# One kernel of attention and two feed-forward layers, with all its instructions in another program order

## The chip, the cores and the metric

The kernel runs on one core of one Trainium2 chip. The metric is the device time of one execution in microseconds (us). The core has a matrix engine (TensorE, PE in the rows; PEld is its weight load), a vector engine (DVE), a scalar engine (ACT), GpSimd (POOL) and a sync engine (SP), whose queue issues nearly all DMA transfers here (SPq in the rows). Each engine takes its instructions in the order in which the program lists them; an instruction that waits for another engine holds up all that stand behind it on its own.

## The reference

```
attn = window attention: q_l, k_l, v_l (4, 8, 512, 64), 32 global rows q_g, k_g, v_g per head
       (local rows see |i - j| <= 32 and the global rows; global rows see all; softmax with max)
x    = attn as (2176, 512)                                       # 4 * (512 + 32) rows
h    = max(max(x @ w1, x @ w2), x @ w3);  x = h @ w_out          # w1..w3 (512, 768), w_out (768, 512)
out  = (sigmoid(x @ w_gate) * (x @ w_val)) @ w_out2              # (512, 1536), (1536, 512)
```

All is float32. w1 to w_out2 arrive as float64, two 32-bit words for a number.

## The kernel before, in words

**Attention** goes by 32 units `t` of one batch, one half of the sequence and one pair of heads (labels "sc" scores, "sm" softmax, "av" the product with v; "smg", "avg" for the global rows, whose scores are `sgs`, maxima and sums `stg` and exponents `eg`). The first eight units (batch 0) transpose on TensorE.

**The max layer** goes by 8 chunks `c` of 256 or 288 rows. For each of six slabs `f` of 128 hidden columns and each of w1 to w3, `moe1_l1` (L877) makes one product into one of three PSUM banks (L882 for chunk 0, whole float32; L321 to L323, three products of high and low parts, for the others); ACT (L890) or DVE (L893, L896) takes it out into `h32`, of which there are two buffers. `moe1_l2` (L909) multiplies by w_out (L918 for chunk 0): one product goes through slabs 0 to 5 of w_out in that order. In the other chunks ACT rounds the high part (L901) and POOL subtracts for the low one (L271), which is the last reader of an `h32` buffer.

**The weights** of this layer come in 24 pieces, `conv_a(i)` (L297): i from 0 to 17 is w1, w2, w3 of slab i // 3, and 18 to 23 are slabs 0 to 5 of w_out. A piece is one load of 512 KB (L302, L305), then four passes of `to_f32` (L281) that make a float32 of a float64: L285 on ACT (even i) or L287 on DVE (odd i), L289 on ACT, L291 and L294 on DVE. Chunk 0 uses what L294 writes. Then ACT rounds (L312) and POOL subtracts (L271) for the chunks after it.

**The gated layer** (`l3_prod` L1023: seven products for each of 36 units, with `snap` L1044 and `l3_out` L1057 to L1065 taking them out) and **the output layer** (`l4_first` L1202, `l4_prod` L1225) follow. Their weights and inputs are prepared by `w_prep` (L985 on), `wo_pre`, `x_prep` (L949, with DVE and ACT passes at L978 and L976) and `g_prep`.

**What sets the order.** Every step of every part is an event. `put` and `once` collect the events with a nominal time; then a table, `ORDER`, says in which order they are carried out, and this order is the program order of each engine:

```
    order = [e[1] for e in sorted(ev, key=lambda e: e[:2])] if ORDER is None else ORDER
    assert sorted(order) == list(range(len(ev)))
    with tc.manual_schedule():
        for n in order:
            ev[n][2]()
```

Buffers are handed out and waits are set as this order makes them needed. The two steps of `moe1_l2` for one output tile `m` are slabs 0 to 4 and then slab 5:

```
        for f in range(NF1):
            if f == NF1 - 1:
                yield
            h = hold["h", f]
```

Of the kernel before, what the change touches and what calls it, by code (L numbers as in the profile page):

```python
# [22 lines left out]
    0, 57, 56, 62, 58, 63, 64, 65, 66, 5, 6, 59, 67, 68, 69, 70, 71, 7, 161, 162, 74, 8, 75, 76, 77, 95, 96, 1861,  # L23
    1862, 72, 163, 164, 165, 166, 1863, 1826, 1827, 1854, 128, 195, 97, 98, 78, 1855, 79, 167, 80, 81, 9, 168, 10, 194,
    169, 170, 173, 60, 1864, 99, 100, 129, 101, 130, 102, 103, 1828, 87, 82, 171, 131, 1829, 104, 1833, 120, 1856,
    1857, 132, 133, 1847, 1896, 107, 83, 121, 122, 84, 1858, 108, 109, 231, 232, 110, 88, 89, 111, 105, 112, 198, 174,
    73, 175, 113, 176, 106, 199, 177, 11, 12, 1840, 61, 186, 13, 14, 1865, 178, 114, 90, 91, 200, 201, 153, 1903, 154,
    123, 155, 279, 15, 16, 115, 116, 117, 172, 1868, 134, 1889, 135, 136, 118, 119, 202, 187, 156, 137, 179, 124, 125,
    188, 233, 1834, 140, 141, 1830, 1848, 1875, 142, 143, 85, 144, 180, 181, 1910, 203, 208, 1831, 157, 234, 235, 182,
    126, 183, 184, 1832, 209, 196, 223, 86, 145, 280, 204, 205, 206, 1849, 92, 1841, 1842, 93, 146, 147, 256, 207, 148,  # L30
    1843, 236, 185, 127, 149, 210, 1850, 1851, 224, 17, 1904, 150, 1897, 1898, 1899, 241, 151, 152, 225, 1882, 257,
    1852, 1835, 189, 190, 281, 1952, 237, 238, 1853, 258, 191, 192, 239, 240, 1866, 94, 158, 159, 160, 1836, 211, 1917,
    1890, 1900, 212, 1876, 197, 138, 213, 242, 1938, 1837, 214, 215, 282, 283, 337, 284, 1877, 1891, 139, 1869, 193,
    1878, 1326, 1322, 1892, 1323, 1905, 1844, 1879, 1880, 243, 1859, 259, 244, 1893, 1906, 338, 339, 1324, 1325, 1327,
    1328, 1314, 1315, 216, 1881, 226, 1845, 1867, 217, 1860, 312, 285, 313, 218, 219, 286, 264, 314, 315, 1894, 1316,
    289, 1895, 287, 245, 288, 246, 247, 1883, 1838, 1931, 1907, 227, 1839, 1338, 316, 317, 248, 291, 292, 265, 1932,
    1870, 396, 249, 250, 1339, 1901, 1918, 318, 1902, 319, 320, 1911, 251, 252, 1340, 1341, 1912, 220, 221, 1884, 1342,
    266, 222, 1933, 267, 1871, 1872, 1885, 304, 1343, 228, 1939, 229, 321, 293, 290, 1330, 360, 1940, 362, 1846, 305,
    1331, 363, 364, 324, 325, 294, 365, 253, 366, 230, 1924, 1332, 367, 1908, 326, 327, 268, 1, 1925, 254, 1926, 1973,
    340, 1913, 1886, 260, 1887, 255, 261, 1953, 262, 1954, 1914, 1909, 1980, 1333, 398, 399, 295, 1941, 269, 270, 271,  # L40
    296, 341, 1981, 400, 401, 1346, 328, 1959, 1317, 1888, 1334, 1318, 1945, 297, 1335, 1919, 18, 1927, 1942, 298, 299,
    468, 1928, 1934, 1350, 1974, 1935, 1347, 1319, 1320, 368, 306, 1354, 1920, 1960, 322, 1975, 19, 402, 403, 1946,
    1947, 1921, 1348, 1321, 2, 1929, 329, 369, 20, 21, 370, 371, 323, 345, 330, 263, 331, 372, 22, 23, 404, 1355, 300,
    272, 273, 274, 24, 1329, 361, 1948, 1966, 1349, 1961, 1962, 1982, 332, 1983, 1984, 1351, 275, 1987, 1930, 25, 1949,
    1344, 1345, 26, 276, 277, 278, 27, 432, 333, 1356, 307, 334, 335, 308, 1955, 336, 373, 1956, 1957, 1958, 388, 1967,
    375, 376, 405, 470, 471, 1968, 472, 1357, 301, 302, 377, 406, 407, 408, 378, 1358, 1359, 389, 1976, 411, 1988, 412,
    342, 28, 346, 1336, 379, 380, 1352, 1353, 4, 1989, 374, 1990, 1991, 3, 1337, 303, 347, 348, 349, 343, 1963, 413,
    1360, 1361, 309, 1985, 1986, 344, 1969, 1970, 1977, 1374, 1362, 434, 435, 310, 1375, 1376, 1366, 414, 350, 351, 29,
    381, 1370, 1371, 382, 1372, 1873, 1367, 352, 383, 353, 1377, 390, 504, 384, 385, 391, 311, 1874, 354, 409, 355,
    1368, 1363, 356, 1992, 386, 357, 1993, 436, 437, 438, 439, 440, 441, 473, 474, 415, 442, 443, 358, 1369, 1364, 359,  # L50
    445, 416, 444, 1964, 1965, 447, 417, 1978, 1386, 1387, 1378, 1922, 418, 419, 397, 424, 1388, 506, 420, 392, 421,
    1380, 1389, 1979, 448, 449, 450, 507, 475, 387, 476, 425, 422, 426, 427, 481, 477, 478, 1379, 678, 508, 509, 451,
    1923, 1381, 510, 479, 480, 483, 1390, 1391, 1392, 1915, 1393, 452, 1936, 1937, 1382, 1383, 511, 512, 1384, 410,
    591, 593, 453, 454, 1385, 594, 1394, 1395, 433, 484, 595, 1396, 485, 1397, 455, 456, 596, 457, 460, 540, 1971, 597,
    458, 513, 514, 423, 515, 516, 1916, 1398, 1410, 1943, 461, 462, 598, 463, 1399, 1972, 393, 1402, 1403, 459, 486,
    482, 487, 446, 488, 394, 1400, 1401, 1411, 542, 1404, 599, 543, 519, 544, 469, 489, 490, 491, 1414, 1405, 464,
    1944, 492, 493, 517, 496, 494, 465, 395, 1412, 520, 497, 1413, 1415, 498, 1416, 428, 499, 1418, 1406, 1407, 600,
    429, 518, 1950, 1417, 545, 601, 1420, 546, 627, 629, 602, 603, 630, 631, 1951, 521, 632, 522, 1373, 1365, 1422,
    1408, 606, 607, 495, 1419, 1421, 466, 430, 431, 523, 608, 524, 1423, 1409, 1424, 1425, 30, 525, 633, 609, 526, 527,
    505, 634, 532, 528, 547, 548, 680, 500, 553, 529, 714, 533, 554, 1426, 1427, 530, 1428, 549, 550, 551, 552, 555,  # L60
    501, 502, 1438, 556, 531, 534, 576, 1439, 681, 682, 577, 1430, 467, 557, 635, 610, 503, 558, 559, 578, 560, 561,
    562, 1429, 683, 579, 1431, 1432, 563, 1466, 640, 1440, 716, 604, 1467, 717, 1442, 1444, 535, 564, 541, 536, 1443,
    611, 612, 613, 718, 565, 566, 568, 1445, 636, 637, 569, 1446, 1468, 1434, 1469, 1447, 1441, 570, 571, 638, 639,
    684, 537, 538, 539, 719, 720, 614, 1470, 615, 1435, 1450, 605, 1436, 567, 1474, 572, 1471, 1472, 580, 581, 582,
    1433, 642, 685, 616, 592, 583, 584, 686, 1448, 1449, 1451, 786, 619, 1473, 617, 687, 618, 1452, 1453, 688, 689,
    620, 621, 622, 623, 1458, 1459, 641, 573, 1460, 643, 644, 645, 1461, 646, 647, 574, 575, 585, 586, 648, 31, 32, 33,
    690, 1462, 1463, 1454, 649, 1464, 650, 1455, 34, 1476, 35, 1456, 1484, 36, 651, 652, 587, 1465, 1475, 1477, 721,
    722, 663, 727, 37, 38, 653, 39, 588, 693, 40, 41, 589, 723, 724, 590, 628, 691, 655, 656, 664, 665, 1478, 1479,
    1480, 694, 666, 1486, 1457, 657, 658, 667, 695, 1481, 696, 697, 1482, 1483, 728, 624, 1485, 788, 698, 625, 1487,
    1488, 1498, 750, 752, 668, 1494, 1489, 1499, 669, 1490, 1491, 753, 1437, 725, 659, 654, 699, 700, 701, 754, 626,  # L70
    726, 789, 790, 702, 1500, 679, 706, 755, 756, 757, 758, 763, 1492, 707, 708, 660, 661, 729, 670, 671, 764, 730,
    1502, 731, 822, 42, 732, 662, 703, 672, 673, 1503, 674, 1501, 733, 709, 675, 676, 1495, 1496, 677, 704, 759, 760,
    761, 762, 765, 1506, 1507, 766, 767, 768, 1530, 734, 1531, 1508, 1509, 1510, 735, 715, 742, 705, 1511, 743, 736,
    824, 737, 825, 1534, 826, 858, 744, 745, 1532, 1512, 791, 792, 738, 1533, 793, 769, 1535, 827, 770, 1513, 1536,
    771, 828, 794, 860, 772, 1537, 861, 862, 863, 1522, 1493, 710, 739, 909, 711, 712, 713, 773, 774, 775, 1504, 1538,
    1540, 776, 795, 796, 797, 798, 1539, 1541, 801, 829, 746, 751, 1514, 692, 778, 779, 1515, 830, 802, 803, 804, 777,
    945, 740, 831, 780, 832, 833, 805, 1516, 1517, 911, 834, 1518, 1519, 1497, 1542, 781, 787, 806, 864, 865, 866,
    1543, 947, 807, 1520, 741, 1544, 808, 1545, 1521, 809, 810, 871, 912, 913, 837, 838, 839, 840, 914, 782, 783, 784,
    1546, 1523, 43, 1524, 872, 814, 835, 811, 812, 813, 867, 868, 1526, 869, 836, 1525, 870, 841, 815, 894, 873, 874,
# [1397 lines left out]
```

## Time and profile before

| | |
|---|---|
| time, median of 3 runs | 837.06 us (834.76 to 839.17) |
| the profiled execution: its time | 835.94 us |
| its span, from the first instruction to the last | 834.2 us |
| TensorE busy, and its mean granted clock | 803.0 us, 0.986 of full |
| DVE, ACT, POOL busy | 603.9, 470.4, 149.2 us |

The span is 1.74 us shorter than the time of the same execution; what lies around it is not seen in the trace. The profiled execution is 1.12 us below the median.

### The profile page before, as it was taken

To read this page: it belongs to the slowest core of one execution; us is meant where nothing else is said; L and a number is where in the kernel's file an instruction comes from. 1 tells how busy PE (TensorE), PEld (TensorE's weight loads), DVE (VectorE), ACT (ScalarE), POOL (GpSimd) and SP (SyncE) were. 2 spreads that over 40 slices of the span, in tenths; PEclk is the share of its full clock that TensorE was granted. 3 is DMA by queue.
4 is the path that set the end of the run, shared out by engine and by line. 5 is a ranking of instruction groups with operands and counts; after the bars stand their busy time and mean duration, and the time that the engine had idled before them with its cause. 6 is when DMAs were issued, how large, how long until landed. Compare 5 with 4: busy or idle time off the path is not lost.

```text
span 834.2 us, 18134 instructions
## 1 busy us (share of the span) xinstructions
PE 803.0 (96%) x6854; PEld 755.6 (91%) x6854; DVE 603.9 (72%) x1303; ACT 470.4 (56%) x1119; POOL 149.2 (18%) x149
## 2 busy tenths in 40 slices
PE   6989699999999999999999999999999999999998
PEld 4768489998989988899999999999999998999998
DVE  5778957756677666875586978989775669987872
ACT  6786556745555555564546766575645366544441
POOL 3142336433323233423140000000000000000000
PEclk9898799999999999999999999999999999999999
DMA  9976435634544555445344345967342369635311
GB/s 204 268 191 184 102 72 99 107 77 98 102 89 87 95 105 111 95 92 93 141 139 134 124 144 171 306 206 240 121 139 70 127 195 350 200 114 171 121 39 44
DMA packets 217590, 116.07 MB, mean 139 GB/s; under 512 B 161056, under 2 KB 204576, under 8 KB 217504
## 3 DMA queue, kind: packets, MB, share of 16 engines
q1 hardware_dynamic: 216960, 114.80, 50.8%
q8 instruction: 53, 0.87, 0.4%
q14 instruction: 33, 0.27, 0.1%
q10 hardware_dynamic: 544, 0.13, 0.1%
HBM read 74.91 MB, written 28.57 MB: 124 GB/s over the span
## 4 chain that ended last, share of the span: by engine, by line
PE 76%; DVE 7%; SPq 6%; DMA 6%; ACT 2%; issue 2%; POOL 1%; POOLq 0%; DVEq 0%; ACTq 0%
PE pa L1038 16%; PE pa L1225 8%; PE ps L321 8%; PE pe L1038 8%; PE ps L323 7%; PE ps L322 7%; PE pe L1225 4%; PE pb L1038 4%; PE pb L1225 2%; DMA m<-in_moe_w_dram 2%; PE sp L619 2%; PE ps L882 2%; SPq L513 2%; PE ps L918 2%; PE ot L780 1%
## 5 line engine op out<-in xcount | busy, mean ns | idle before, releaser
L1038 PE MATMUL pa<-m,m 128*128 128x384 f32 (+1 forms) x864 | 155.5, 327 | 0.9 <-ACT sn L1044 0.9
L321 PE MATMUL ps<-xt,m 128*128 128x288 f32 (+1 forms) x504 | 149.2, 296 | 5.0 <-DVE h L896 3.8
L323 PE MATMUL ps<-xt,m 128*128 128x288 f32 (+1 forms) x504 | 146.6, 291 | 0.0
L1038 PEld LDWEIGHTS pa<-m,m 128*128 128x128 f32 x864 | 144.4, 188 | 2.1 <-ACT sn L1044 2.0
L322 PE MATMUL ps<-xt,m 128*128 128x288 f32 (+1 forms) x504 | 145.1, 288 | 0.0
L321 PEld LDWEIGHTS ps<-xt,m 128*128 128x128 f32 x504 | 94.7, 188 | 12.7 <-DVE h L896 4.8
L322 PEld LDWEIGHTS ps<-xt,m 128*128 128x128 f32 x504 | 94.8, 188 | 0.0
L323 PEld LDWEIGHTS ps<-xt,m 128*128 128x128 f32 x504 | 94.7, 188 | 0.0
L1044 ACT COPY sn<-pa 128x384 f32<-128x384 f32 (+1 forms) x108 | 49.8, 461 | 61.6 <-PE pa L1038 61.3
L1038 PE MATMUL pe<-m,m 128*128 128x384 f32 (+1 forms) x432 | 83.4, 327 | 0.4 <-ACT m L1207 0.4
L1038 PEld LDWEIGHTS pe<-m,m 128*128 128x128 f32 x432 | 72.8, 188 | 0.9 <-ACT m L1207 0.6
L1225 PE MATMUL pa<-m,m 128*128 128x256 f32 x576 | 72.0, 283 | 0.0
L1225 PEld LDWEIGHTS pa<-m,m 128*128 128x128 f32 x576 | 70.4, 192 | 0.0
L896 DVE TENSOR_TENSOR h<-ps,h 128x288 f32<-128x288 f32 (+1 forms) x90 | 38.9, 437 | 40.5 <-PE ps L323 32.8
L661 ACT ACTIVATE sm<-sm,st 128x224 f32<-128x224 f32 x128 | 60.6, 475 | 9.5 <-DVE st L625 9.4
L1163 ACT CAST m<-m 128x768 fp32r<-128x768 f32 x44 | 36.6, 836 | 44.1 <-PE pa L1225 13.9
L271 POOL TENSOR_TENSOR h<-h,h 128x288 fp32r<-128x288 f32 (+1 forms) x42 | 42.1, 1004 | 92.7 <-ACT h L901 88.7
L707 DVE TENSOR_TENSOR pc<-sm,pc 64x512 f16<-64x512 f32 (+1 forms) x72 | 51.5, 715 | 6.6 <-ACT pc L704 5.7
L1168 DVE TENSOR_TENSOR m<-m,m 128x768 fp32r<-128x768 f32 x44 | 41.5, 956 | 18.2 <-ACT m L1163 17.4
L321 PE MATMUL ps<-h,m 128*128 128x288 f32 (+1 forms) x168 | 50.3, 300 | 0.0
L704 ACT CAST pc<-sm 64x512 f16<-64x512 f32 (+1 forms) x72 | 39.2, 545 | 18.0 <-DVE sm L675 17.2
L322 PE MATMUL ps<-h,m 128*128 128x288 f32 (+1 forms) x168 | 48.5, 289 | 0.6 <-POOL h L271 0.6
(194 smaller groups left out, 1632.4 us busy)
## 6 DMA issues: line engine op xcount, KB each, us to landing
m<-in_moe_w_dram SPq DMA_DIRECT2D x18, 512.0 KB, 5.7
gd<-sgt SPq DMA_DIRECT2D x48, 192.0 KB, 2.6
m<-gd SPq DMA_DIRECT2D x6, 1536.0 KB, 8.2
m<-in_moe_w_val_dram SPq DMA_DIRECT2D x6, 1024.0 KB, 5.2
wr<-in_moe_w_out_dram SPq DMA_DIRECT2D x6, 1024.0 KB, 6.3
m<-in_moe_w_gate_dram SPq DMA_DIRECT2D x5, 1024.0 KB, 5.4
vr<-in_v_l_dram SPq DMA_DIRECT2D x48, 96.0 KB, 2.5
x2d<-x2s SPq DMA_DIRECT2D x32, 128.0 KB, 1.9
```

Source lines behind the costliest of these rows:

```text
L271: nc.gpsimd.tensor_tensor(out=out, in0=a, in1=f32(b), op=ALU.subtract)
L321: nc.tensor.matmul(ps, lhsT=wh, rhs=xh, start=first, stop=False)
L322: nc.tensor.matmul(ps, lhsT=wh, rhs=xl, start=False, stop=False)
L323: nc.tensor.matmul(ps, lhsT=wl, rhs=xh, start=False, stop=last)
L661: nc.scalar.activation(sm4[:, i], sm4[:, i], AF.Exp, bias=st[:, 0, i:i + 1], scale=-1.0, accum_out=st[:, 2, i:i + 1])
L704: nc.scalar.copy(d, s_)
L707: nc.vector.tensor_tensor(out=l_, in0=s_, in1=h_, op=ALU.subtract)
L896: nc.vector.tensor_tensor(out=a, in0=ps[:, 0:n], in1=a, op=ALU.max)
L1038: nc.tensor.matmul(ps, lhsT=w[l][:, a, i], rhs=x[m][:, i], start=(k in (1, 2, 5) and i + l + m == 0), stop=(k in (2, 3, 4) and i == 1 and ...
L1044: nc.scalar.copy(t[:, 0:n], pend[u]["a"][:, 0:n])
L1168: tt(out=lo, in0=src[op], in1=f32(hi), op=ALU.subtract)
L1225: nc.tensor.matmul(ps, lhsT=g[l][:, f], rhs=wo_op(b, f, m), start=(k in (1, 2, 5) and f + l + m == 0), stop=(k in (2, 3, 4) and f == 5 and ...
```

## The change

The 3388 numbers of `ORDER` stand in another order; nothing else is changed. 3291 places of the table hold another event than before, and an event stands 19 places from where it stood, in the mean. Instructions, sizes and loads are the same ones; names of buffers are numbered anew in program order.

```
 ORDER = [
-    0, 57, 56, 62, 58, 63, 64, 65, 66, 5, 6, 59, 67, 68, 69, 70, 71, 7, 161, 162, 74, 8, 75, 76, 77, 95, 96, 1861,
...
+    2380, 2381, 3372, 2387, 2303, 3373, 2388, 2389, 2390, 2304, 2391, 2392,
 ]
```

The first place is DVE where TensorE begins the w_out product of chunk 0. Before: slabs 1, 2, 3 and 5 of w_out are m42_889, m45_1057, m39_839 and m46_1072; stg and eg are global rows 7, sm_991 is the softmax of unit 8, xt_1168 the rounding of unit 7.

```order
L724 TENSOR_SCALAR stg_1001<-stg_1001 128x1
L667 RECIPROCAL st_992<-st_992 128x4
L675 TENSOR_TENSOR sm_991<-sm_991,st_992 128x896
L291 SCALAR_TENSOR_TENSOR m46_1072<-m46_1072 128x512
L294 SCALAR_TENSOR_TENSOR m46_1072<-m46_1072 128x512
L731 RECIPROCAL stg_1001<-stg_1001 128x1
L733 TENSOR_SCALAR eg_1002<-eg_1002,stg_1001 128x640
L294 SCALAR_TENSOR_TENSOR m42_889<-m42_889 128x512
L798 SCALAR_TENSOR_TENSOR xt_1168<-ot_1136,xt_1168 128x256
L291 SCALAR_TENSOR_TENSOR m45_1057<-m45_1057 128x512
L294 SCALAR_TENSOR_TENSOR m45_1057<-m45_1057 128x512
L294 SCALAR_TENSOR_TENSOR m39_839<-m39_839 128x512
```

Now slab 2 is m46_1013, slab 3 is m40_821 and slab 5 is m45_1010 (slab 1 is done 26 rows earlier than slab 2, outside these rows), on DVE at the same place:

```order
L291 SCALAR_TENSOR_TENSOR m40_821<-m40_821 128x512
L291 SCALAR_TENSOR_TENSOR m46_1013<-m46_1013 128x512
L294 SCALAR_TENSOR_TENSOR m46_1013<-m46_1013 128x512
L569 STREAM_TRANSPOSE qt_1110<-qr_1023 128x256
L572 STREAM_TRANSPOSE kt_1112<-kgr_527 128x2x32
L574 STREAM_TRANSPOSE kt_1112<-kr_1024 128x64
L576 STREAM_TRANSPOSE kt_1112<-kr_1024 128x2x128
L294 SCALAR_TENSOR_TENSOR m40_821<-m40_821 128x512
L287 TENSOR_SCALAR m45_1010<-m45_1010 128x512
L896 TENSOR_TENSOR h32_1062<-ps1_1088,h32_1062 128x256
L667 RECIPROCAL st_998<-st_998 128x4
L675 TENSOR_TENSOR sm_997<-sm_997,st_998 128x896
```

Twelve steps that stood ahead of slab 3's L294 now stand behind it: L287, L291 and L294 of slab 5, L667 and L675 of unit 8, L731 and L733 of the global rows, L896 and L893 of the last slab of the first layer, two of the score steps (L625) of unit 9, and L798 of unit 7. None has moved ahead of it.

The second place is DVE some 50 us earlier. Before: m35_695 is piece 15 (w1, slab 5) and m27_560 piece 13, the L625 rows are the scores of unit 7.

```order
L724 TENSOR_SCALAR stg_671<-stg_671 128x1
L287 TENSOR_SCALAR m35_695<-m35_695 128x512
L287 TENSOR_SCALAR m27_560<-m27_560 128x512
L625 ISA sm_741,st_742<-sp_704,mask_79 128x224
L625 ISA st_742 128x1
```

Now piece 15 is m36_741 and piece 13 m27_561; L688 takes out transposed softmax:

```order
L287 TENSOR_SCALAR m27_561<-m27_561 128x512
L688 COPY pw_713<-tp_707 128x512
L625 ISA sm_733,st_734<-sp_726,mask_79 128x224
L625 ISA st_734 128x1
L625 ISA sm_733,st_734<-sp_726,mask_79 128x224
L625 ISA st_734 128x1
L625 ISA sm_733,st_734<-sp_727,mask_79 128x224
L625 ISA st_734 128x1
L625 ISA sm_733,st_734<-sp_727,mask_79 128x224
L625 ISA st_734 128x1
L287 TENSOR_SCALAR m36_741<-m36_741 128x512
```

Piece 13, the copy of unit 5 and the four score steps of unit 7 moved ahead of piece 15's first pass. On SP's queue the load of piece 15 moved one place ahead, past that of piece 16, and the load of piece 10 moved from the third of the group issued at 21.9 us to just behind that of piece 8.

The third place is ACT near the end of the max layer, in its last chunk. Before: h_6615 rounds slab 2 (L901), h32_6679 takes out the first product of slab 0 (L890).

```order
L925 COPY x2s_6613<-ps2_6569 128x256
L901 CAST h_6615<-h32_6478 128x288
L976 CAST m75_6619<-m64_6489 128x768
L976 CAST m77_6627<-m60_6442 128x768
L925 COPY x2s_6643<-ps2_6593 128x256
L890 COPY h32_6679<-ps1_6650 128x288
```

Now, with h_6690 for slab 2 and h32_6693 for slab 0:

```order
L289 ACTIVATE m59_6424<-m59_6424 128x1024
L976 CAST m75_6629<-m64_6550 128x768
L976 CAST m77_6634<-m60_6468 128x768
L901 CAST h_6638<-h32_6545 128x288
L925 COPY x2s_6657<-ps2_6612 128x256
L901 CAST h_6690<-h32_6440 128x288
L890 COPY h32_6693<-ps1_6641 128x288
```

The rounding of slab 2 moved behind the casts of `x_prep` and the rounding of slab 1, and stands right ahead of the copy for slab 0.

## Rows read from the trace of the kernel before

**Rows 1.** Windows: busy us and count of each engine, granted clock, DMA share, GB/s.

```profile
0.00:58.00 58.00, 48.17 (x300) 36.48 (x300) 38.45 (x114) 43.72 (x135) 19.28 (x35) 0.94 0.93 233
58.00:118.00 60.00, 49.10 (x337) 39.53 (x337) 47.35 (x117) 32.58 (x91) 15.12 (x12) 0.86 0.47 117
118.00:450.00 332.00, 326.09 (x3670) 303.43 (x3670) 231.62 (x632) 186.99 (x534) 114.82 (x103) 1.00 0.48 99
450.00:831.00 381.00, 379.59 (x2552) 376.20 (x2550) 286.13 (x443) 207.13 (x361) 0.00 (x0) 1.00 0.50 164
```

**Rows 2.** Timeline of PE, 58 to 118 us: start, duration, instructions, idle before and releaser.

```profile
61.97 6.71 PE L882 MATMUL ps<-xw,m 128*128 128x256 f32 x16 [2.83 <-DVE m L294]
...
70.24 5.35 PE L882 MATMUL ps<-xw,m 128*128 128x256 f32 x24
...
92.79 0.71 PE L918 MATMUL ps<-hw,m 128*128 128x256 f32 x2
100.31 1.22 PE L918 MATMUL ps<-hw,m 128*128 128x256 f32 x2 [6.81 <-DVE m L294]
102.78 7.67 PE L918 MATMUL ps<-hw,m 128*128 128x256 f32 x28 [1.26 <-issue]
...
117.74 0.40 PE L321 MATMUL ps<-xt,m 128*128 128x288 f32 x1
```

**Rows 3.** Windows of PE alone, around the first long wait: busy, clock, DMA.

```profile
60.00:65.00 5.00, 3.03 (x7) 0.62 0.57 125
65.00:70.00 5.00, 5.00 (x29) 0.70 0.86 261
```

**Rows 4.** Timeline of DVE, 92 to 104 us.

```profile
92.37 0.38 DVE L896 TENSOR_TENSOR h<-ps,h 128x256 f32<-128x256 f32 x1
...
94.94 1.37 DVE L287 TENSOR_SCALAR m<-m 128x512 int32<-128x512 uint32 x1
...
96.30 0.16 DVE L667 RECIPROCAL st<-st 128x4 f32<-128x4 f32 x1
...
99.57 0.68 DVE L294 SCALAR_TENSOR_TENSOR m<-m 128x512 int32<-128x512 int32 x1
100.17 0.42 DVE L798 SCALAR_TENSOR_TENSOR xt<-ot,xt 128x256 fp32r<-128x256 f32 x1
...
101.99 1.29 DVE L294 SCALAR_TENSOR_TENSOR m<-m 128x512 int32<-128x512 int32 x2
```

**Rows 5.** Timeline of DVE, 53 to 58 us.

```profile
53.43 0.14 DVE L724 TENSOR_SCALAR stg<-stg 128x1 f32<-128x1 f32 x1
57.91 0.76 DVE L287 TENSOR_SCALAR m<-m 128x512 int32<-128x512 uint32 x2 [4.34 <-DMA m<-in_moe_w_dram]
```

**Rows 6.** Timeline of SP's queue, 40 to 50 us: the load of piece 8.

```profile
45.03 0.43 SPq L302 DMA_DIRECT2D m<-in_moe_w_dram  x1
```

**Rows 7.** The line L302 from 20 to 60 us: time to landing.

```profile
DMA to landing us min/median/max: 3.7/6.1/9.3
```

**Rows 8.** The page's costliest groups: busy, mean ns of one, idle before.

```profile
L704 ACT CAST pc<-sm 64x512 f16<-64x512 f32 (+1 forms) x72 | 39.2, 545 | 18.0 <-DVE sm L675 17.2
```

**Rows 9.** Timeline of DVE, 103 to 118 us.

```profile
111.03 0.29 DVE L744 COPY pwg<-tpg 128x128 f32<-128x128 f32 x1 [6.82 <-PE tpg L738]
```

**Rows 10.** Timeline of POOL, 395 to 450 us.

```profile
404.12 0.74 POOL L271 TENSOR_TENSOR h<-h,h 128x256 fp32r<-128x256 f32 x1 [6.30 <-ACT h L901]
416.68 5.24 POOL L271 TENSOR_TENSOR h<-h,h 128x288 fp32r<-128x288 f32 x1 [11.81 <-ACT h L901]
```

**Rows 11.** Timeline of ACT, 405 to 430 us.

```profile
421.95 0.40 ACT L890 COPY h<-ps 128x288 f32<-128x288 f32 x1 [3.59 <-POOL h L271]
```

**Rows 12.** Waits of PE from 450 us on: us in total, times, longest.

```profile
PE pa L1038 <- ACT sn L1044: 0.9, 3, 0.4
PE pe L1038 <- ACT m L1207: 0.4, 1, 0.4
```

**Rows 13.** Waits of SP's own queue over the span: us in total, times, longest.

```profile
SPq L928 <- ACT x2s L925: 61.5, 15, 14.3
```

338 rows, old and new, of the table ORDER are left out of this document.

## The prediction

> **What bounds the kernel now.** I read the windows by stage first [rows 1]. TensorE is busy 803.0 of 834.2 us, so the reader should look for where it is idle, since a change of order alone can take nothing else away. From 0 to 58 us it idles 9.8 us, from 58 to 118 us 10.9, from 118 to 450 us 5.9, from 450 to 831 us 1.4. The first two stretches are 14% of the span and hold two thirds of the idle time; the second also runs at a mean granted clock of 0.86. The last stretch, the gated and output layers, is TensorE work with hardly a gap. The waits of TensorE there [rows 12] are 0.9 and 0.4 us. Whatever the new order does to ACT and DVE there can win about 1 us.
>
> Then I read the timeline of TensorE from 58 to 118 us [rows 2]. Two places wait. At 59.1 us the third product of slab 0 of chunk 0 waits 2.83 us for a weight that DVE finishes with L294, and the 16 matmuls behind it take 6.71 us. At full clock 24 such matmuls take 5.35, so 16 take 3.57: 3.1 us are lost to the clock, which the windows show at 0.62 and 0.70 after the wait [rows 3], between the levels of 1.2 and 2.4 GHz. At 93.5 us the w_out product of chunk 0 waits 6.81 us, starts one tile, and waits 1.26 more: slabs 1, 2 and 3 of w_out come from DVE's L294 one after another, and the last one starts at 101.99 and ends at 103.28 [rows 4]. The 28 matmuls behind it take 7.67 us, where the full rate gives 28 x 0.223 = 6.24, so another 1.4 us are lost. Chunk 1 (L321) can only start at 117.74.
>
> The timeline of DVE shows why the weights are late. From 92 to 103 us it has no idle time [rows 4]: it works, in program order, through steps that nobody waits for before it comes to slab 3. Behind slab 3, with chunk 0 done, it idles 6.82 us at 111.03 [rows 9], so what is put off there has room. Earlier it stood idle 4.34 us for the load of piece 15, up to 57.91 [rows 5], with piece 13 and four score steps queued behind.
>
> **The change, part by part.** The sum is made against the profiled execution, 835.94 us, which is 1.12 below the median of the runs.
>
> *Twelve DVE steps go behind slab 3's L294.* L287 of slab 5 takes 1.36 from its start to the next (94.94 to 96.30); the six consecutive steps L667, L675, L291, L294, L731 and L733 take 3.27 (96.30 to 99.57) [rows 4]. The other five (L896, two of L625, L893, L798) are short; the first and the last of them last 0.38 and 0.42 and overlap their neighbours, so I take 0.32 each, 1.6 together. The sum is 6.2. DVE is dense there, so slab 3 is done 6.2 us earlier. The wait is 6.81 + 1.26 = 8.07, so 1.9 of it stays and the whole 6.2 counts. The product is started by slab 3 in both orders, since slab 5 is used by a second step. The steps put off cost nothing where DVE's idle 6.82 [rows 9] takes them; L291 and L294 of slab 5 are still due before the end of the product, and run while TensorE works its 7 us on slabs 0 to 4. **-6.2.**
>
> *The clock behind that wait.* A shorter wait may lose less. Nothing here shows a wait of 1.9 us in this stretch, so the bounds are 0 (the loss stays 1.4) and -1.4. I take half, **-0.7**. The row of the 2.83 us wait, after which 3.1 were lost [rows 2, 3], speaks against taking it all. The Trainium skill (TensorE: Matmul & The Clock Gate, Part 1: The HAM clock gate) says that throttled is the default state and that activity releases it; the low clock after both waits agrees (0.62 after the first), and by that rule a remaining gap may still be paid for, which is one of the rivals below.
>
> *The load wait of DVE.* Piece 13's first pass (0.76 [rows 5]), a copy and four score steps now stand ahead of piece 15's first pass, and its load is issued one place earlier. Of the wait of 4.34 [rows 5] that can recover up to all. Against it, piece 10's load now follows piece 8's, which is issued at 45.03 [rows 6]; with the median time to landing of 6.1 [rows 7] it is there at 51.1, and two ACT passes stand between it and DVE. That can make DVE wait 1 to 3.4 us in the same stretch. Net I take **-2.0**, bounds 0 and -4.3. DVE is dense from 74 us on, so this goes through to slab 3.
>
> *A new chain behind slab 5.* The reciprocal of global rows 7 (L731) now stands behind slab 5's L294 and waits for an exponential on ACT, which stands behind the copies of unit 8 (L704, 0.545 each [rows 8]). With two of them that is 1.1 us and more, on the way to the last attention product before chunk 1; DVE also has L291 and L294 of slab 5 and some short steps ahead of that product's last step, of the kinds costed above, which I put at 1.7 together. Against that stands the idle 6.82 of DVE [rows 9]. Bounds 0 and 1.1 + 1.7 = +2.8; I take **+1.0**.
>
> *ACT and POOL in the last chunk.* Of `h32` there are two buffers; the copy L890 of slab 0 waits 3.59 for POOL's L271 of slab 2 [rows 11], which takes 5.24 in place of 0.74 when it lies beside a dense run of DVE [rows 10]. It ends just before TensorE needs the bank, and so costs nothing now. In the new order L901 of slab 2 stands last before that copy, behind casts that nobody waits for. If POOL starts that much later, TensorE waits, from 0 up to about the 3.4 that ACT's wait is today. I take **+0.5**, nearer to nothing.
>
> *The gated layer.* A product of the output layer is put ahead of the one that waits 0.4 for ACT's L1207 [rows 12] and covers it: **-0.4**.
>
> *The middle, 118 to 450 us.* TensorE idles 5.9 in all [rows 1], in a handful of waits of 0.5 to 2 us. Every row has moved, by some 19 places in the mean; for each engine the work ahead of a wait changes by tenths of a us up or down. The bounds are -4 (most of the idle goes) and +6 (it doubles); I take **0**.
>
> The sum is -6.2 - 0.7 - 2.0 + 1.0 + 0.5 - 0.4 = -7.8, so 835.94 - 7.8 = 828.1, and with the 1.12 by which the median lies above the profiled execution, **829.2 us**. What this measurement can tell from no change is about 0.5%, 4.2 us: faster means below 832.9, slower above 841.2. The likeliest case's own range is 825 to 832.9: the load wait between 0 and -4.3 and the middle a us or two either way.
>
> **The rivals.**
>
> *More is won.* The whole 4.34 of the load wait is recovered, the wait of 2.83 at 59.1 shrinks with part of its 3.1 of clock loss [rows 2], and the middle loses two of its waits. That is -2.3, -2 and -1 more, 823 to 824. For it speaks that DVE's work before 60 us is reordered too; against it that the first slabs' pieces still go through the same four passes in much the same order. Chance 0.13.
>
> *Half is given back.* Piece 10's late load makes DVE wait the full 3.4 instead of piece 15's, so nothing is won there (+2.0), the clock loss stays (+0.7), and the last chunk waits its full 3.4 (+2.9). With the first alone the time is 831.2, with all three 829.2 + 5.6 = 834.8; with the chain behind slab 5 at its bound too (+1.8) 836.6. The clock alone, if the remaining 1.9 us cost as much as the 2.83 us did (3.1 instead of 0.7), gives 831.6. Chance of 833 to 841: 0.18.
>
> *Slower: SP's queue.* Loads of the next units stand on SP's queue between stores that wait for ACT; the stores wait 61.5 us in all, 14.3 the longest [rows 13]. Today the loads are issued early enough. If the new order puts loads of several units behind a store that waits longer, TensorE waits for scores between 118 and 400 us. From 8 us in all the gain is gone, and from 12 the kernel is slower: with 24 units from there on, 0.5 us for each makes 829.2 + 12 = 841. The order of SP's queue is nearly the same as before and units are loaded with about the same lead, which speaks against it. Chance 0.10.
>
> *The change doesn't reach slab 3*: another wait, of the first layer's last products, holds slab 3's turn anyway. That gives 834 to 836 and is within the second rival's chance.
>
> **How the numbers follow.** The forecast has 0.59, more won 0.13, half given back 0.18, slower 0.10. Faster by over 0.5% is 0.59 + 0.13 = 0.72, no change 0.18, slower 0.10. The range of 8 in 10 leaves out the slower case and the upper part of the second: 823 to 838.
>
> **What the profile after would show.** Right: the wait ahead of the 28 matmuls of L918 is about 2 us in place of 8; chunk 1's first L321 starts at about 110 (117.74 - 6.2 - 0.7 - 2.0 + 1.0 = 109.8); DVE's idle 4.34 and 6.82 are gone or under 3; TensorE's idle time from there to the gated layer is still about 6, and in the gated and output layers about 1. Wrong: a wait of DVE for piece 10's load at 50 us that is as long as piece 15's was; a wait on L731 or L733 in front of chunk 1; a wait for L890 in the last chunk near its slab 0; TensorE waiting for scores or loads of units in the middle. The prediction fails most easily if the 6 us are won in front and the middle or the last chunk, where every row has moved, returns them in waits of 1 to 2 us that no single row of the trace before announces.

## The result and the profile after

The changed kernel took 826.92 us (median of 4 runs, 826.33 to 829.82) beside 836.05 for the kernel before in the same session: ratio 0.9892, 95% interval 0.9864 to 0.992. A second session gave 0.9856 (0.9832 to 0.9879). 829.2 had been forecast, with a range of 823 to 838. The profiled execution has a span of 825.2 us against 834.2, so 9.0 us less, of which TensorE's busy time gives 5.8 (797.2 against 803.0) and its idle time 3.2.

To see where they come from, the two executions are cut at the same places of the program: the first L918 of chunk 0, the first L321 of chunk 1, the last L321 that reads `h`, and the end. These are windows of TensorE of the kernel before (window, length, busy, granted clock, DMA share, GB/s):

```profile
0.00:92.79 92.79, 80.14 (x525) 0.93 0.83 208
92.79:117.74 24.95, 16.89 (x111) 0.79 0.21 46
117.74:448.60 330.86, 324.95 (x3664) 1.00 0.48 100
448.60:834.20 385.60, 380.99 (x2561) 1.00 0.49 162
```

And of the changed kernel:

```profile
0.00:91.37 91.37, 78.88 (x526) 0.98 0.83 212
91.37:107.66 16.29, 15.20 (x112) 1.00 0.35 74
107.66:442.70 335.04, 324.26 (x3671) 0.99 0.47 98
442.70:825.20 382.50, 378.82 (x2554) 1.00 0.50 164
```

Six L1038 stand in the third window after and in the fourth before; they take 1.0 us. With that set right, the start gives 1.4 us, the w_out product of chunk 0 and what leads to chunk 1 give 8.7, the middle takes 3.2 back, and the gated and output layers give 2.1: 1.4 + 8.7 - 3.2 + 2.1 = 9.0.

The traces of the runs below say how firm these are. The second stage took 24.95 to 26.5 us in four executions with the order of before there (before, e2_rest, e3b_gated, e5_piece15) and 16.2 to 16.5 in six with the new one: this is the gain. The 1.4 of the start is not shown: the first L918 came at 90.1 to 93.0 us in six executions whose order up to there is that of before or moves piece 15 alone, and at 91.1 to 95.2 in five with the new one.

The timeline of TensorE after, at the places of [rows 2]:

```profile
54.34 1.09 PE L683 MATMUL tp<-ident,sm 128*128 128x128 f32 x8 [2.76 <-DVE sm L675]
...
63.20 3.73 PE L882 MATMUL ps<-xw,m 128*128 128x256 f32 x16 [0.28 <-DVE m L294]
...
93.55 3.30 PE L918 MATMUL ps<-hw,m 128*128 128x256 f32 x14 [0.61 <-DVE m L294]
97.14 6.29 PE L918 MATMUL ps<-hw,m 128*128 128x256 f32 x28 [0.29 <-issue]
103.45 0.77 PE L738 MATMUL tpg<-ident,eg 128*128 128x128 f32 x5
...
107.66 0.40 PE L321 MATMUL ps<-xt,m 128*128 128x288 f32 x1
```

The waits of 6.81 and 1.26 are now 0.61 and 0.29, the 28 matmuls run at full rate (6.29 for 6.24), and chunk 1 starts at 107.66 where 109.8 was forecast. The wait of 2.83 ahead of piece 6 is 0.28, but one of 2.76 for a softmax (L675) stands at 54 us. In DVE's timeline that L675 takes 2.17 us, where before it took 1.08; POOL works on its L271 beside it, up to 53.3 us:

```profile
52.11 2.17 DVE L675 TENSOR_TENSOR sm<-sm,st 128x896 f32<-128x896 f32 x1
```

The timeline of DVE after, at the places of [rows 4]: slab 3's L294 is done at 93.50 in place of 103.28.

```profile
92.85 0.65 DVE L294 SCALAR_TENSOR_TENSOR m<-m 128x512 int32<-128x512 int32 x1
93.42 0.42 DVE L287 TENSOR_SCALAR m<-m 128x512 int32<-128x512 uint32 x1
...
98.39 0.17 DVE L731 RECIPROCAL stg<-stg 128x1 f32<-128x1 f32 x1 [1.35 <-ACT stg L729]
...
102.85 0.55 DVE L733 TENSOR_SCALAR eg<-eg,stg 128x640 f32<-128x640 f32 x1
```

Windows of DVE up to the end of slab 3, and from 50 to 74 us, first of the kernel before, then of the changed one:

```profile
0.00:103.28 103.28, 79.98 (x218) 0.90 0.76 192
50.00:74.00 24.00, 15.24 (x47) 0.86 0.85 227
```

```profile
0.00:93.50 93.50, 78.37 (x204) 0.98 0.82 208
50.00:74.00 24.00, 21.75 (x53) 0.93 0.69 190
```

Slab 3 comes 9.8 us earlier; only 1.6 of it is busy time, and 8.2 is idle time that DVE no longer has ahead of this place (23.3 before, 15.1 after), 6.5 of it between 50 and 74 us. (That window is one of fixed microseconds. In e2_rest, e4_slabs and e9_both, whose order there is that of before or nearly so, DVE works 18.0 to 18.4 us in it, so some 3 of the 6.5 lie between executions.) The busy time fell by less than the steps that moved behind, since some others took longer beside POOL, among them this L675 and a copy (L410, 1.97 for 0.27); the last experiment comes to that.

The middle after, where TensorE waits (timeline):

```profile
150.63 0.82 PE L780 MATMUL ot<-pt,vb 128*64 128x64 f16 x40 [1.66 <-DVE st L625]
158.79 0.39 PE L321 MATMUL ps<-xt,m 128*128 128x256 f32 x1 [1.38 <-ACT xt L796]
160.61 0.39 PE L322 MATMUL ps<-xt,m 128*128 128x256 f32 x1 [1.43 <-DVE xt L798]
...
223.12 0.61 PE L321 MATMUL ps<-xt,m 128*128 128x288 f32 x1 [2.79 <-ACT h L890]
```

Its idle time is 10.8 us (335.04 - 324.26) where it was 5.9.

### The profile page after: what moved, and what is told of

Read it like the earlier page. It is cut to its first block, busy times and chain, and to the rows that moved or that the text cites. A ratio compares the mean times of both kernels' runs of the same rounds, so it can differ in the third digit from the quotient of the medians.

```text
span 825.2 us, 18078 instructions
## 1 busy us (share of the span) xinstructions
PE 797.2 (97%) x6854; PEld 757.4 (92%) x6854; DVE 610.4 (74%) x1303; ACT 467.0 (57%) x1119; POOL 150.0 (18%) x149
## 4 chain that ended last, share of the span: by engine, by line
PE 71%; DVE 10%; SPq 5%; ACT 5%; DMA 4%; issue 3%; POOL 1%; DVEq 0%; ACTq 0%; POOLq 0%
PE pa L1038 17%; PE pe L1038 8%; PE pa L1225 8%; PE ps L321 6%; PE ps L322 5%; PE ps L323 5%; PE pe L1225 4%; PE pb L1038 4%; PE sp L619 3%; DMA vr<-in_v_g_dram 2%; PE pb L1225 2%; PE ps L882 2%; ACT sm L661 2%; DVE m L978 2%; PE ot L780 1%
## 5 line engine op out<-in xcount | busy, mean ns | idle before, releaser
L321 PE MATMUL ps<-xt,m 128*128 128x288 f32 (+1 forms) x504 | 149.4, 296 | 6.9 <-ACT h L890 4.0
L1038 PE MATMUL pa<-m,m 128*128 128x384 f32 (+1 forms) x864 | 155.7, 327 | 0.3 <-ACT sn L1044 0.3
L1038 PEld LDWEIGHTS pa<-m,m 128*128 128x128 f32 x864 | 144.5, 188 | 0.8 <-ACT sn L1044 0.6
L321 PEld LDWEIGHTS ps<-xt,m 128*128 128x128 f32 x504 | 96.0, 191 | 11.8 <-ACT h L890 5.2
L322 PEld LDWEIGHTS ps<-xt,m 128*128 128x128 f32 x504 | 96.1, 191 | 2.4 <-DVE xt L798 2.0
L323 PEld LDWEIGHTS ps<-xt,m 128*128 128x128 f32 x504 | 96.0, 190 | 0.0
L1038 PE MATMUL pe<-m,m 128*128 128x384 f32 (+1 forms) x432 | 82.0, 327 | 0.0
L1038 PEld LDWEIGHTS pe<-m,m 128*128 128x128 f32 x432 | 72.6, 188 | 0.0
L896 DVE TENSOR_TENSOR h<-ps,h 128x288 f32<-128x288 f32 (+1 forms) x90 | 39.0, 435 | 40.2 <-PE ps L323 28.9
L707 DVE TENSOR_TENSOR pc<-sm,pc 64x512 f16<-64x512 f32 (+1 forms) x72 | 54.2, 752 | 8.0 <-ACT pc L704 6.7
L271 POOL TENSOR_TENSOR h<-h,h 128x288 fp32r<-128x288 f32 (+1 forms) x42 | 41.4, 990 | 90.1 <-ACT h L901 86.1
L625 DVE CUSTOM_DVE_ANT_0 sm<-sp,mask 128x224 f32<-128x224 f32 x128 | 44.7, 383 | 11.1 <-PE sp L619 10.3
L704 ACT CAST pc<-sm 64x512 f16<-64x512 f32 (+1 forms) x72 | 39.2, 546 | 18.4 <-DVE sm L675 16.7
L321 PE MATMUL ps<-h,m 128*128 128x288 f32 (+1 forms) x168 | 49.5, 295 | 0.0
```

The lines of the kernel that those rows point to most:

```text
L271: nc.gpsimd.tensor_tensor(out=out, in0=a, in1=f32(b), op=ALU.subtract)
L321: nc.tensor.matmul(ps, lhsT=wh, rhs=xh, start=first, stop=False)
L322: nc.tensor.matmul(ps, lhsT=wh, rhs=xl, start=False, stop=False)
L323: nc.tensor.matmul(ps, lhsT=wl, rhs=xh, start=False, stop=last)
L625: nc.vector.tensor_tensor_reduce(out=sm[:, hh, j], in0=sp[hh][:, j, 0:224], in1=mask[:, half + j, :], scale=-SC, scalar=3.0e38, op0=ALU.ad ...
L704: nc.scalar.copy(d, s_)
```

## The experiments

All are orders of the same events; none leaves out or changes a part of the computation. Ratios are to the kernel before, run beside each. The numbers in the diffs are those of `ORDER`.

**e1_front and e2_rest: each half of the new order alone.** The first takes the new order up to the first event of chunk 1 and then what is left in the order of before; the second is the reverse.

```diff
 e1_front: the new order up to
     1979, 357,
+    119, 336, 301, 302, 374,      (what is left, as before)
 e2_rest: the order of before up to
     417, 1978,
+    640, 475, 387, 397,           (what is left, in the new order)
```

> The new order up to the first matmul of chunk 1, and behind it what is left in the order of before. Theory (the gain is made in front, and the middle gives 3 us of it back in waits of its own): chunk 1 starts at about 107.7 us as in the changed kernel, and with the old middle its waits of 5.9 us in all come back in place of 10.8, so the time is 10 us below that of before, ratio 0.988, or 1 us below the changed kernel. Rival (the middle's waits follow from what the front leaves behind, whatever the order there): TensorE idles 10 us in the middle here too, and the time is 5 to 7 us below before, ratio 0.992 to 0.994.

> The old order up to the first matmul of chunk 1, and behind it what is left in the new one. Theory: nothing is won in front, the middle costs 3 us and the gated part gives 2 back: 1 us above before, ratio 1.001 (0.998 to 1.005). Rival (the new middle is as good as the old, and its waits come from starting 10 us earlier): 2 us below before, ratio 0.998 and the idle time of TensorE from chunk 1 to the gated part is about 6 us.

e1_front: ratio 0.9897 (0.9876 to 0.9918). e2_rest: 0.9971 (0.9952 to 0.9991). The windows of the middle and of the layers behind it, of e1_front and of e2_rest:

```profile
107.30:440.00 332.70, 325.88 (x3667) 1.00 0.48 99
440.00:825.60 385.60, 380.97 (x2561) 1.00 0.49 162
```

```profile
117.60:447.90 330.30, 322.32 (x3669) 0.99 0.49 100
447.90:830.30 382.40, 378.91 (x2555) 1.00 0.49 164
```

The front holds nearly the whole gain, as expected, and TensorE idles 6.8 us in the middle of e1_front, nearer to the theory's 5.9 than to the rival's 10. But in e2_rest the rival comes nearer: the new middle behind the old front takes 330.3 us, or 329.3 without the six L1038, less than the old one (330.86), while behind the new front it takes 335.0 (334.0). So its extra waits are not in its order alone. Nor do they go by the time at which it starts: in e6_undo12, below, it starts 5.7 us later than in the changed kernel and takes the same 334.9. That the old middle behind the new front takes 332.7 says little, since that order took 330.4 to 333.9 behind the old front (before, e5_piece15, e3b_gated, e12_pool). e2_rest is 2 us faster than before in the time as well, and most of that lies in the gated part (383.4 with the six L1038, against 385.6).

**e3_front_gated and e3b_gated: the three stages recombined.** The first is e1_front with the new order again from the first event of the gated layer; the second changes nothing but that part.

```diff
 e3_front_gated and e3b_gated, behind 2979, 2980:
-    1997, 1824, 2981, 1812,
+    2981, 2982, 2983, 1812, 1813,   (what is left, in the new order)
```

> New order up to the first matmul of chunk 1, the order of before for the middle, and the new one again from the first product of the gated layer on. Theory (three stages whose times nearly add): front as in the changed kernel, middle 2 us shorter than there, as in the run with the new front alone, and the gated part 2 us shorter than before: 11 to 12 us below before, ratio 0.986 to 0.987, the fastest of these orders. Rival (the middle's difference between the two orders is chance of the clock): the same as the changed kernel, ratio 0.989 to 0.990.

> The order of before up to the first product of the gated layer, and behind it what is left in the new order. Theory: the weight loads of TensorE's queue there waited 2.0 us for ACT's L1044 and 0.6 for L1207, of which 1.9 go: the stretch behind the max layer is 2 us shorter and the time 2 us below before, ratio 0.9975, which five rounds may just tell. Rival (only what TensorE itself waited goes, 1 us): ratio 0.999.

e3_front_gated: 0.9883 (0.9862 to 0.9904), e3b_gated: 0.9988 (0.997 to 1.0006). The two theories of each cannot be told apart in the times. The windows can: behind the last L321 of `h`, e3b_gated takes 383.6 us and e3_front_gated 382.9, where six executions with the old order of that part (before, e1_front, e4_slabs, e5_piece15, e9_both, e12_pool) took 384.6 to 386.2. The groups of TensorE's weight loads in this stretch show what went, first before, then in e3b_gated (busy, mean ns, idle time ahead and its releasers):

```profile
L1038 PEld LDWEIGHTS pa<-m,m 128*128 128x128 f32 x864 | 144.4, 188 | 2.1 <-ACT sn L1044 2.0
L1038 PEld LDWEIGHTS pe<-m,m 128*128 128x128 f32 x432 | 72.8, 188 | 0.9 <-ACT m L1207 0.6 <-DVE m L1020 0.3
```

```profile
L1038 PEld LDWEIGHTS pa<-m,m 128*128 128x128 f32 x864 | 144.6, 188 | 0.8 <-ACT sn L1044 0.7
L1038 PEld LDWEIGHTS pe<-m,m 128*128 128x128 f32 x432 | 72.6, 188 | 0.0
```

2.1 + 0.9 - 0.8 = 2.2 us less waiting at the weight loads, and 2.0 less time (385.6 to 383.6). The waits of the matmuls [rows 12] show only 1.3 of it. A wait is longer in the rows of the weight loads than in those of the matmuls: two waits of e4_slabs are 2.42 and 2.00 in the one and 2.02 and 1.63 in the other. In the times themselves e3b_gated is not shown to be faster than before.

**e4_slabs: in the order of before, slabs 1 to 3 ahead of the twelve steps.**

```diff
     1976,                           (slab 3, L291)
+    1963, 1969, 1970, 1977,         (slab 1 L294; slab 2 L291, L294; slab 3 L294)
+    1357, 407, 408, 1359,           (L896, two L625, L893)
```

> The order of before with one edit: the last DVE steps of slabs 1, 2 and 3 of w_out ahead of the twelve steps that the change put behind them. Theory (the 6.2 us of steps were the wait): the waits of 6.81 and 1.26 us ahead of the w_out product fall to 1 to 2 us in all, the 28 matmuls behind them take 6.2 to 7.7, and the time is 6 to 7.5 us below before, ratio 0.991 to 0.993. Rival (the steps put off are waited for at once, as the twelve lie on the way to chunk 1): chunk 1 starts less than 3 us earlier, ratio 0.997 to 1.000.

Ratio 0.9937 (0.9913 to 0.9961). TensorE's timeline:

```profile
92.84 0.71 PE L918 MATMUL ps<-hw,m 128*128 128x256 f32 x2 [2.02 <-DVE m L294]
95.17 7.72 PE L918 MATMUL ps<-hw,m 128*128 128x256 f32 x28 [1.63 <-ACT m L289]
```

The waits fall from 8.07 to 3.65, and the product and what leads to chunk 1 take 20.1 us in place of 24.95. The rival (a start of chunk 1 less than 3 us earlier) falls: 110.2 in place of 117.74. But the theory's 1 to 2 us of waiting were missed, and with them its time. The row names ACT's L289 for the second wait, but no L289 on ACT lies between 94.5 us and TensorE's start at 95.17; that start falls where the first of DVE's two L294 from 94.38 on (slab 2) is done. What made DVE late are POOL's steps beside it (DVE, then POOL):

```profile
91.14 1.64 DVE L294 SCALAR_TENSOR_TENSOR m<-m 128x512 int32<-128x512 int32 x1
92.71 1.64 DVE L291 SCALAR_TENSOR_TENSOR m<-m 128x512 int32<-128x512 int32 x1
94.38 1.29 DVE L294 SCALAR_TENSOR_TENSOR m<-m 128x512 int32<-128x512 int32 x2
```

```profile
90.63 1.61 POOL L593 TENSOR_TENSOR vr<-vr,vb 128x512 f32<-128x512 f32 x1
92.31 1.49 POOL L418 TENSOR_TENSOR vs<-vgr,t 32x512 bf16<-32x512 f32 x1
```

The L294 of slab 1 and the L291 of slab 2 take 1.64 where such steps take 0.69 elsewhere, and slab 3's L291 ahead of them 1.26. An estimate from these rows: the three lose 2.5 us, which leaves 1.2 of the 3.65. The clock gave nothing back either: the 28 matmuls take 7.72, as long as behind the wait of 8.07.

**e6_undo12: the reverse, in the changed kernel.** Slab 3's L294 goes behind the steps again.

```diff
-    1977,                           (slab 3, L294)
...
+    1988, 1357, 1989, 379, 380, 1359, 1990, 1991, 347, 348, 349, 407, 408, 344,
+    1977,
     1374,                           (w_out product)
```

> The changed kernel with one edit: slab 3's L294 on DVE stands again behind the steps that the change put behind it (L287, L291 and L294 of slab 5, L667 and L675 of unit 8, L731 and L733, the takings-out, score steps and L798). Theory: slab 3 is late by these 6.2 us and TensorE waits 6 to 8 us ahead of the w_out product in place of 0.9, with 1.4 of clock behind it: 6 to 8 us above the changed kernel, ratio to before 0.997 to 0.999. Rival (the gain came from DVE no longer standing idle ahead of this place, and not from the steps): at most 3 us above the changed kernel, ratio 0.990 to 0.993.

Ratio 0.9932 (0.9909 to 0.9955), against 0.9892 and 0.9856 for the changed kernel. DVE's row of slab 3 and TensorE's row behind it:

```profile
97.93 0.68 DVE L294 SCALAR_TENSOR_TENSOR m<-m 128x512 int32<-128x512 int32 x1
```

```profile
98.67 10.93 PE L918 MATMUL ps<-hw,m 128*128 128x256 f32 x42 [5.80 <-DVE m L294]
```

Slab 3 is 5.1 us later (97.93 against 92.85), TensorE waits 5.80 in place of 0.90 in all, and the 42 matmuls take 10.93 where the changed kernel needs 3.30 + 6.29 = 9.59 for them: 4.9 + 1.3 = 6.2 us. Chunk 1 starts 5.7 us later (113.35). The wait is just under what was expected (5.80 for 6 to 8) and the clock's share is about as expected (1.3 for 1.4); the ratio lies between the two theories, 3 to 6 us above the changed kernel, by which of its two sessions one takes (6 by the second, which ran on the chip of e6_undo12).

**e5_piece15 and e9_both: the load wait of DVE.** In the order of before, DVE's first pass of piece 15 goes behind piece 6's last; e9_both has this and the edit of e4_slabs.

```diff
-    1932,                           (piece 15, L287, behind 265)
...
-    1933,                           (piece 15, L289 on ACT)
...
     1872,                           (piece 6, L294)
+    1932, 1933,
```

> The order of before with one edit: DVE's first pass of piece 15 (and the ACT pass behind it) is put behind the last step of piece 6; no load is moved. Theory: DVE no longer stands 4.34 us for the load at 53.6; the steps up to piece 6 come about 2 us earlier, the wait of 2.83 us at 59.1 shrinks to about 1, and with it part of the 3.1 us that the clock cost behind it; the w_out product's wait shrinks by about as much as DVE is ahead: 2 to 5 us below before in all, ratio 0.994 to 0.998. Rival (DVE's idle time there is covered later, so that slab 3 comes no earlier): the time is within 1 us of before.

> The order of before with both earlier edits: the steps of slabs 1 to 3 put forward, and DVE's pass of piece 15 put behind piece 6. Theory (between 50 and 74 us DVE is paced by TensorE, so that the time saved on the load is idled away at the next matmul): as with the slabs alone, ratio 0.992 to 0.995, and DVE idle in 50 to 74 us is as long as there within 1 us. Rival (the two add): 2 us or more below the slabs alone, ratio 0.989 to 0.991.

e5_piece15: 1.0003 (0.9985 to 1.0021). e9_both: 0.9937 (0.9917 to 0.9958), just as e4_slabs alone. The timeline of DVE in e5_piece15 shows where the 4.34 us went:

```profile
57.80 0.16 DVE L731 RECIPROCAL stg<-stg 128x1 f32<-128x1 f32 x1 [1.46 <-ACT stg L729]
64.05 0.45 DVE L569 STREAM_TRANSPOSE qt<-qr 128x256 f32<-128x256 f32 x1 [3.19 <-issue]
74.11 0.42 DVE L893 TENSOR_TENSOR hw<-ps,h 128x256 f32<-128x256 f32 x1 [2.77 <-PE ps L882]
```

The load wait is gone, and DVE idles 1.46, 3.19 and 2.77 at the next places; for the 3.19 the profile shows no releaser. From 50 to 74 us it works 15.70 us, as before (15.24), and 18.36 in e4_slabs and e9_both alike. The wait for piece 6 falls from 2.83 to 0.77, but TensorE then waits 1.89 for the global rows (L733), and 24 matmuls behind that take 8.05 for 5.35. Slab 3 is no earlier: TensorE waits 6.81 and 1.25 for it. In e5_piece15 the rival holds, in e9_both the theory: taken alone, or with the slabs, this wait is worth nothing in the time.

**e11_after_front and e10_two_more: two further waits.** e11_after_front is the changed kernel with the softmax of unit 5 ahead on DVE; e10_two_more is e3_front_gated with that and with one taking-out of the fourth chunk ahead of five other steps.

```diff
-    1899,                           (piece 10, L291)
...
-    287, 288,                       (two L625)
...
     247,                            (unit 5, L667)
-    1907,                           (piece 11, L294)
     248,                            (unit 5, L675)
+    1899, 287, 288, 1907,
 e10_two_more, also:
     1524,
+    1525,                           (L896 of that product, ahead of five other steps)
```

> The changed kernel with the first of these two edits alone. Theory: the wait of 2.76 us at 54 us goes, and the clock that was granted at 0.71 and 0.86 behind it is full: chunk 1 starts 2 to 4 us earlier, and of that 1 to 4 reach the end, ratio to before 0.985 to 0.988. Rival (the pieces put off, or TensorE's waits in the middle, take it back): ratio 0.988 to 0.990.

> The mixed order (new front, old middle, new gated part) with two more edits on DVE, each read from a wait of TensorE: the softmax of unit 5 (L667, L675) ahead of a piece's L291 and L294 and two score steps, since TensorE waits 2.74 us for it at 54 us; and one taking-out (L896) in the fourth chunk ahead of two L707 and three score steps, since TensorE waits 1.95 us for it near 243 us. Theory (a wait whose releasing step stands behind others that are not due is worth its length and the clock behind it): both waits fall under 0.5, the clock stays full from 56 to 62 us, and the time is 3 to 5 us below the mixed order, ratio to before 0.982 to 0.985. Rival (the matmuls behind the first wait are then held by the weight pieces put off): at most 2 us below it, ratio 0.986 to 0.988.

> The changed kernel unchanged, as the measure for the two others on the same chip: ratio to before 0.986 to 0.992.

e11_after_front: 0.985 (0.9826 to 0.9874); e10_two_more: 0.9874 (0.9859 to 0.9888); the changed kernel beside them 0.9856 (0.9832 to 0.9879). TensorE in e11_after_front:

```profile
53.18 1.09 PE L683 MATMUL tp<-ident,sm 128*128 128x128 f32 x8 [0.95 <-DVE sm L675]
55.51 1.72 PE L619 MATMUL sp<-kw,qw 64*128 64x224 f32 x6 [0.67 <-DVE st L625]
...
64.47 3.73 PE L882 MATMUL ps<-xw,m 128*128 128x256 f32 x16 [1.39 <-DVE m L294]
```

The one wait of 2.76 became three of 0.95, 0.67 and 1.39, and chunk 1 starts at 108.3, where the changed kernel starts it at 107.7 and 107.9. So the theory of e11_after_front, an earlier chunk 1, falls: what was put off is waited for next, and two of its L291 take 1.8 us beside POOL. In e10_two_more the rival's time holds too; there the waits are 1.07, 0.66, 0.66 and 2.13, and the wait of 1.95 in the fourth chunk fell only to 1.07. None of these versions is shown to be faster than the changed kernel.

**e12_pool: POOL's work away from DVE's last weight steps.** In the order of before, the ACT steps that release three POOL steps go behind the first copies of the w_out product.

```diff
-    1957, 1958,                     (L312 on ACT, L271 on POOL)
...
-    388, 389,                       (L591 on ACT, L593 on POOL)
...
-    1985, 1986,                     (L312, L271)
...
     351,                            (L742 on ACT)
+    1957, 1958, 388, 389, 1985, 1986,
```

> The order of before with one edit: the ACT steps (two L312, one L591) that release POOL's two L271 and its L593 between 92 and 101 us are put behind the first copies of the w_out product, so that POOL works after slab 3 and not beside DVE's last weight steps; DVE's order is untouched. Theory (in before these POOL steps lengthen the DVE steps beside them: L291 1.08 and 1.45, L287 1.37 us, where alone they take 0.7 and 0.4): the three take 0.7, 0.4 and 0.7, slab 3 is done 1.5 to 2.5 us earlier, the waits of 8.07 us ahead of the w_out product are 6 to 6.6, and the time is 1 to 2.5 us below before, ratio 0.997 to 0.999. Rival (these DVE steps are long for another reason): the three keep their durations and the wait its length.

Ratio 1.0018 (0.9997 to 1.0039): no faster. The DVE steps did what was expected. POOL before, then DVE in e12_pool, both by the timeline:

```profile
93.32 1.16 POOL L593 TENSOR_TENSOR vr<-vr,vb 128x512 f32<-128x512 f32 x1
94.55 1.48 POOL L418 TENSOR_TENSOR vs<-vgr,t 32x512 bf16<-32x512 f32 x1
99.60 1.80 POOL L271 TENSOR_TENSOR m<-m,m 128x512 fp32r<-128x512 f32 x1 [3.57 <-ACT m L312]
```

```profile
97.26 0.68 DVE L291 SCALAR_TENSOR_TENSOR m<-m 128x512 int32<-128x512 int32 x1
97.86 0.42 DVE L287 TENSOR_SCALAR m<-m 128x512 int32<-128x512 uint32 x1
...
102.47 0.68 DVE L291 SCALAR_TENSOR_TENSOR m<-m 128x512 int32<-128x512 int32 x1
```

L287 takes 0.42 and not 1.37 [rows 4], and the two L291 0.68. The waits ahead of the product are 6.22 + 0.48 = 6.7 in place of 8.07, and the product with what leads to chunk 1 takes 23.8 us in place of 24.95. But a wait of 1.74 us for another weight piece came up at 82 us, the first L918 only started at 95.3, and the middle took 333.9 us. The wait at 82 us is no price of the edit, since every engine's order is that of before up to there: DVE stood 2.09 us for a load (L393) up to 80.15, and an L294 behind it took 1.81 beside POOL. For the middle this run doesn't tell the price of the steps put off from what differs between executions. So the rows show 1.2 us won at this place, and the times of 12 runs show none of it.

## Why the prediction was right

The sign, the place and the size were right (-7.8 forecast on the profiled execution, -9.0 measured), but the terms were not all right; that the sum came so near is in part luck, since 2.1 us more than forecast were won up to chunk 1 and 1.7 more in the gated part, and the middle took 3.2 back. One premise was wrong from the start: that a change of order can take away nothing but idle time. TensorE's busy time gave 5.8 of the 9.0, part of it by the clock, which the prediction itself priced.

- **Twelve DVE steps, -6.2.** The mechanism is shown from both sides, by e4_slabs and e6_undo12. The size was 5.1 us of DVE time in e6_undo12, mostly because L287 was taken at 1.36 from a row in which POOL worked beside it; free of that it is 0.42.
- **The clock behind that wait, -0.7.** All of it came: 7.67 to 6.29, -1.4. The step that failed is "1.9 of it stays": 0.9 stayed. (The sum was at odds with itself here: 6.2 and the 2.0 of the load wait, both taken from a wait of 8.07, would have left nothing.) Half was a guess, and a wait of 1.9 might have won nothing: behind 3.65 and 3.67 us of waiting in e4_slabs and e9_both the 28 matmuls took 7.72 and 8.92, behind 8.05 to 8.07 in before, e2_rest, e3b_gated and e5_piece15 7.67 to 9.22, and behind 0.85 to 1.08 in six executions with the new order 6.29.
- **The load wait, -2.0.** The failed step is "DVE is dense from 74 us on, so this goes through to slab 3". By e5_piece15 and e9_both, the wait alone is worth nothing, since DVE then waits for TensorE and for other inputs. In the changed kernel slab 3 did come earlier by more than the twelve steps. Counted from the first L918 it is done 10.5 us behind it before, 7.3 in e6_undo12 and 2.1 in the changed kernel: 5.2 for the twelve steps and 3.2 for the rest of the new front. Part of the 3.2 is POOL, which no term has: before, L287 and two L291 ahead of slab 3 lost 2.1 us beside its steps, and in the changed kernel POOL has none from 89.1 to 97.4 us. e12_pool, which moves POOL's steps alone, shortened the waits by 1.4. Which moves did the rest stays open. Piece 10's late load cost nothing: DVE has no idle time at its L291 at 49.3 us.
- **The chain behind slab 5, +1.0.** The wait is there, 1.35 us at L731, but L733 ends at 103.40 and TensorE comes to L738 at 103.45 with no wait. The term is 0. With this 1.0, the clock's 0.7 and 0.4 more of waits and start, chunk 1 started 2.1 us earlier than forecast.
- **ACT and POOL in the last chunk, +0.5.** TensorE waits for neither there; the 0.59 that it waited for POOL at 441 us is gone. ACT's L890 waits 1.42 for L271 and not 3.59.
- **The gated layer, -0.4.** It gave 2.1. The step that failed is the price, which was taken from the waits of the matmuls [rows 12]: the weight loads waited 2.6 us for ACT there, and most of that went.
- **The middle, 0 with -4 to +6.** It cost 3.2, and TensorE idles 10.8 us there where "still about 6" was the sign of being right. The bounds held; the forecast's own warning, that waits of 1 to 2 us would return some of the gain, is what happened. Behind the new front the old middle takes 332.7, 331.8 and 331.4 us (e1_front, e3_front_gated, e10_two_more), the new one without its six L1038 334.0, 332.7, 333.6 and 333.9 (changed kernel, its repeat, e11_after_front, e6_undo12). So the new order costs about 1.6 us more there than the old one would (means of 333.6 and 332.0). The other 1.1 (332.0 against 330.86) is not told from what the old order shows behind the old front, 330.4 to 333.9. Why the new middle waits longer behind the new front than in e2_rest stays open: e6_undo12 speaks against the earlier start by itself, and e2_rest is one execution.

Of the rivals, the one on SP's queue is excluded: TensorE waits for no load of a unit between 118 and 400 us. The rival that a shorter wait costs as much clock is not tested by the changed kernel, whose remaining waits at that place are under 1 us; the two executions with 3.65 and 3.67 us, above, bear it out.

## What to carry to other kernels

A wait of the bounding engine that is released by the last of a row of steps is worth the steps ahead of it that nobody waits for, and the clock behind it if the wait nearly goes (here at 0.9 us, not at 3.65); price such steps from rows in which no other engine worked beside them, and look at which steps a new order puts beside each other. An idle stretch of a helper engine is worth nothing by itself: look what it meets next before it is added to the sum. The stage behind an order change can return some of the gain (here 3.2 us). Measure stages between the same points of the program, not between the same microseconds, and in several executions: one order's start and middle differed here by 3 us and more.

## What the runs showed of the hardware

**DVE steps lengthen beside POOL.** In before, L287 and two L291 beside POOL's tensor-tensor steps took 1.37, 1.08 and 1.45 us and in e12_pool, with POOL idle, 0.42, 0.68 and 0.68. L625 and L896 kept 0.37 to 0.39 in both. The lengthened L291 and L294 end 0.5 to 0.6 us after POOL's step (before: 95.02 after 94.48, 101.96 after 101.40; e4_slabs: 92.78 after 92.24, 94.35 after 93.80), a little less than the 0.68 they take alone, as if they began only when POOL was done. The Trainium skill (GPSIMD Engine Reference, 1. Specifications) says that GpSimd's way to SBUF is shared with VectorE, with contention for DVE instructions that have two SBUF inputs or work in a two-port mode; the trace agrees for L291, which has two inputs in SBUF, and for L896, which takes one from PSUM.

**The clock after a wait.** With TensorE's wait ahead of 16 L882 at 0.28, 0.54, 0.64, 0.77, 1.27 and 1.39 us they took 3.73; at 2.13, 2.44, 2.49, 2.68 and 2.83 they took 5.41, 5.42, 5.33, 5.32 and 6.71; but in e12_pool they took 3.73 after a wait of 2.55. In the old middle a wait of 1.95 or 1.96 us stands at the same place of the program in eight executions. The granted clock of the 10 us around it was 0.83 or 0.84 in e3b_gated, e4_slabs and e12_pool, but 1.00 in before, e1_front, e3_front_gated, e5_piece15 and e9_both. So the price of a wait of this length is not the same in each execution. The start of the kernel differs in the same way: up to the first L918 the new order took 91.4 us in the changed kernel and 95.2 in e3_front_gated, where the granted clock was 0.50, the 1.2 GHz level, from 24 to 32 us (1.00 in the changed kernel).
